# A decode layer on one core: w_down in five transfers instead of nine

## The chip, the cores and the metric

The kernel runs on one core of a Trainium2 chip. The metric is the device time of one execution in microseconds (us). A core has a tensor engine (PE in the profile's rows), a vector engine (DVE), a scalar engine (ACT), GpSimd (POOL) and SyncE (SP), each with its own instruction queue; weight loads of the tensor engine stand apart as PEld. All data comes by transfers that an engine's queue issues and sixteen transfer engines carry out, each with a share of every large transfer.

## The reference

One token passes a layer whose attention and gated MLP run in parallel on the same normalised input. All numbers are 32-bit floats. Attention looks at the last 4096 of 65536 cached positions, with 32 query heads on 4 key and value heads of 128.

```
def reference(A_x, A_k_cache, A_v_cache, A_wq, A_wo, B_x, B_w_gate, B_w_up, B_w_down):
    ...
        scores = jnp.einsum("bhqd,bhkd->bhqk", q, k) * (Dh ** -0.5)
        p = _softmax(scores, axis=-1)
        o = jnp.einsum("bhqk,bhkd->bhqd", p, v)
    ...
        g = jnp.einsum("bsd,df->bsf", x, w_gate)
        u = jnp.einsum("bsd,df->bsf", x, w_up)
        h = _gelu(g) * u
        return jnp.einsum("bsf,fd->bsd", h, w_down)
    ...
    xn = _layernorm(x, axis=-1)
    return x + _A_ref(xn, A_k_cache, A_v_cache, A_wq, A_wo) + _B_ref(xn, B_w_gate, B_w_up, B_w_down)
```

What matters here is the last product: a hidden vector h of 3584 numbers times w_down, 3584 x 1024, 14.7 MB.

## The kernel before, in words

Weights and caches are read once, 94 MB in all, and pass through one buffer of 176 KB in each of 128 partitions, `ring`. The list `pieces` names every transfer in order: its kind (q, k, v, g, u, o for the matrices and caches, d for w_down), which part, the place in `ring` in KB and the size in KB a partition. `pump` issues transfers from SyncE in that order, each as soon as no live piece holds its place; a piece ends with `done`. Which instruction waits for what is worked out by `Program.add` from overlapping places, piece of memory by piece of memory, so a transfer waits for the last readers of the bytes that it overwrites.

The vector by matrix products are shared between the two engines. w_down is cut into 28 tiles of 128 rows and 1024 columns (4 KB a partition each). `hz` holds h, one column a tile; `column(t)` is that column among zeros. A tile can be done in three ways:

- `tile_on_dve`: one instruction on the vector engine, `part = part + tile * column` (line 213), for the tile numbers in lists such as `HID_B`.
- `tiles_on_rows` and `tile_on_pe`: four or eight matmul calls a tile on the tensor engine. `tile_on_pe` cuts the 1024 columns into four blocks of 256 and sums into the bank `sums`; each call shows as two matmul records in the trace, so a tile is eight records.
- `half_on_pe`: half of a tile's columns, in four calls of 128 columns (eight records), into the bank `acc`.

All matmul calls stand on line 158, all vector additions on 189, all transfers on 219. `contract` does a whole piece: it gives its listed tiles to the vector engine and the others to the tensor engine.

The tail of the program, around the change: the two pieces of wo, "o" 0 and "o" 1, are done, each half on either engine. Then w_down: piece (0, 12) of 48 KB takes the place that the last piece of w_up left; all others go to the first 64 KB of `ring`, which "o" 0 leaves. (0, 12) is summed by rows in `acc` and on the vector engine in `part`; the vector engine adds `acc` to `part`. Then (12, 20), (20, 22), (22, 24), tile 24, a pass `tile_on_pe(unit, out_part)` that takes the vector engine's sum across the partitions into `sums`, and tile 25 last in `sums`. The vector engine adds `sums` to `x_out`, which holds x. Tiles 26 and 27 go in halves to `acc`: both halves of 26, then half 0 of 27, its addition to `x_out` and the store, then half 1 of 27, its addition and its store. Tile 27 comes in two transfers, one a half.

```
HID_B = [1, 3, 5, 7]
HID_C = []
HID_D = [1]
...
        ("d", (0, 12), 128, 48), ("d", (12, 20), 0, 32), ("d", (20, 22), 32, 8),
        ("d", (22, 24), 40, 8), ("d", (24, 25), 48, 4), ("d", (25, 26), 52, 4),
        ("d", (26, 27), 56, 4), ("d", (27, 28), 60, 4),
```

Of the kernel before, what the change touches and what calls it, by code (L numbers as in the profile page):

```python
# [10 lines left out]
P = 128  # L11
D = 1024
# [4 lines left out]
NQ = 512  # L17
NG = 448
TO = 16
TD = DF // P  # L20
# [7 lines left out]
HEADS_A = [0, 2, 4, 6, 8, 10, 12, 14]  # L28
HEADS_B = [0, 2, 4, 6, 8, 10, 12, 14]
HID_A = [0, 2, 4, 6, 8]  # L30
HID_B = [1, 3, 5, 7]
HID_C = []
HID_D = [1]


class Program:
# [110 lines left out]
def decode_layer(nc, x, k_cache, v_cache, wq, wo, w_gate, w_up, w_down, out):  # L147
    prog = Program(nc)

    def sbuf(name, *shape):  # L150
        return nc.alloc_sbuf_tensor(name, list(shape), F32)
# [4 lines left out]
    def mm(o, lhsT, rhs, start, stop, parts=None):  # L156
        prog.add(
            "pe", lambda e: e.matmul(o, lhsT, rhs, start=start, stop=stop),  # L158
            [lhsT] + (parts or [rhs]), [o],
        )  # L160
# [27 lines left out]
    def add(o, a, b):  # L188
        dve(lambda e: e.tensor_add(o, a, b), [a, b], [o])  # L189
# [27 lines left out]
    def dma(engine, o, i, reads=(), writes=(), tag=None):  # L217
        return prog.add(
            engine, lambda e: e.dma_start(o, i), list(reads), list(writes), dma=True, tag=tag  # L219
        )  # L220
# [4 lines left out]
    def rows(w, a):  # L225
        return w[512 * a:512 * (a + 1), :].rearrange("(p r) n -> p (r n)", r=4)

    def heads_of(a):
        return wo[2048 * a:2048 * (a + 1), :].rearrange("(p t) n -> p (t n)", p=P)

    hidden_rows = w_down.rearrange("(p t) n -> p t n", p=P)


    pieces = [
# [6 lines left out]
    ]  # L241
    held = {}

    def load(kind, i, at, size):
        slot = ring[:, at * KB:(at + size) * KB]
        held[kind, i] = slot
        if kind == "v":
            src = v_cache[0, 2 * i:2 * i + 2, SK - WIN:, :].rearrange("g (p j) d -> p g (j d)", p=P)
            dma("sp", slot.rearrange("p (g n) -> p g n", g=2), src, writes=[slot], tag=(kind, i))
        elif kind == "k":  # L250
            src = k_cache[0, 2 * i:2 * i + 2, SK - WIN:, :].rearrange("g (s j) d -> s g (j d)", g=2, j=64)
            dma("sp", slot, src, writes=[slot], tag=(kind, i))
        elif kind == "d":
            lo, hi = i
            halves = 2 if lo == TD - 1 else 1
            wide = slot.rearrange("p (t n) -> p t n", n=D)
            for half in range(halves):
                cols = slice(half * D // halves, (half + 1) * D // halves)
                dst = wide[:, :, cols]
                dma("sp", dst, hidden_rows[:, lo:hi, cols], writes=[dst], tag=(kind, i, half))  # L260
        else:
            src = {
                "q": lambda: rows(wq, i), "g": lambda: rows(w_gate, i), "u": lambda: rows(w_up, i),
                "o": lambda: heads_of(i),
            }[kind]()
            dma("sp", slot, src, writes=[slot], tag=(kind, i))
# [4 lines left out]
    def pump():  # L271
        while queue:
            kind, i, at, size = queue[0]
            if any(at < hi and lo < at + size for lo, hi in live.values()):
                return
            load(*queue.pop(0))
            live[kind, i] = (at, at + size)

    def done(*key):
        del live[key]  # L280
        pump()
# [8 lines left out]
    for k in range(2):  # L290
        dst = x_out[31 + 64 * k:33 + 64 * k, :, :]
# [22 lines left out]
    unit = sbuf("unit", P, 64)  # L314
# [133 lines left out]
    p = rows_sb[:, 0, :]  # L448
# [152 lines left out]
    out_part = part[:, :D]  # L601
# [3 lines left out]
    def column(t):  # L605
        return hz[:, 32 * t:32 * t + 64]

    def head(t):
        return oz[:, 32 * t:32 * t + 64]

    def tiles_on_rows(pairs):

        for at in range(0, len(pairs), 4):
            group = pairs[at:at + 4]
            for f in range(2):
                for k, (z, w) in enumerate(group):
                    c = (state["turn"] + k) % 4
                    first = (c, f) not in state["rows"]
                    state["rows"].add((c, f))
                    mm(  # L620
                        acc[32 * c:32 * c + 32, f, :], z[:, 31:63], w[:, f * NQ:(f + 1) * NQ],
                        first, state["turn"] + k >= state["total"] - 4,
                    )
            state["turn"] += len(group)

    def tile_on_pe(wide, w, stop=False):
        blocks = w.rearrange("p (f c n) -> p c f n", f=2, c=4)
        for c in range(4):
            at = 31 * (c % 2)
            mm(  # L630
                sums[32 * c:32 * c + 32, :].rearrange("p (f n) -> p f n", f=2),
                wide[:, at:at + 32], blocks[:, c], state["fresh"], stop,
            )
        state["fresh"] = False

    def half_on_pe(wide, w, half, first, last):
        for c in range(4):
            at = 31 * (c % 2)
            mm(
                acc[32 * c:32 * c + 32, half, :P],  # L640
                wide[:, at:at + 32], w[:, half * NQ + c * P:half * NQ + (c + 1) * P], first, last,
            )

    def tile_on_dve(z, w):
        add_scaled(out_part, w, z[:, 31:32], state["part"])
        state["part"] = False

    def contract(kind, i, z, dve_tiles, rows):
        w = held[kind, i].rearrange("p (t n) -> p t n", n=D)
        count = w.shape[1]  # L650
        rest = [(z(t), w[:, t, :]) for t in range(count) if t not in dve_tiles]
        if rows:
            tiles_on_rows(rest)
        else:
            for pair in rest:
                tile_on_pe(*pair)
        for t in dve_tiles:
            tile_on_dve(z(t), w[:, t, :])
        done(kind, i)
# [39 lines left out]
    state["total"] = 2 * TO + 12 - len(HEADS_A + HEADS_B + HID_A)  # L699
    contract("o", 0, head, HEADS_A, True)  # L700
    contract("o", 1, lambda t: head(TO + t), HEADS_B, True)
    contract("d", (0, 12), column, HID_A, True)
    add(out_part, acc[:].rearrange("p a n -> p (a n)"), out_part)
    contract("d", (12, 20), lambda t: column(12 + t), HID_B, False)
    contract("d", (20, 22), lambda t: column(20 + t), HID_C, False)
    contract("d", (22, 24), lambda t: column(22 + t), HID_D, False)
    tile_on_pe(column(24), held["d", (24, 25)])
    tile_on_pe(unit[:], out_part)
    tile_on_pe(column(25), held["d", (25, 26)], True)
    add(x_out[:].rearrange("p f n -> p (f n)"), sums[:], x_out[:].rearrange("p f n -> p (f n)"))  # L710
    for half in range(2):
        half_on_pe(column(26), held["d", (26, 27)], half, True, False)
    stores = out.rearrange("a b (f c n) -> (a b) f c n", f=2, c=4)
    for half in range(2):
        half_on_pe(column(27), held["d", (27, 28)], half, False, True)
        add(y[:, half, :], acc[:, half, :P], x_out[:, half, :])
        for k, engine in enumerate(("sp", "act")):
            src = y[31 + 64 * k:33 + 64 * k, half, :]
            dma(
                engine, stores[0, half, 2 * k:2 * k + 2, :], src, reads=[src],  # L720
                tag=("out", half, k),
            )
# [25 lines left out]
```

## Time and profile before

| what | value |
|---|---|
| median of three runs | 226.62 us (226.55 to 226.67) |
| the profiled execution, its own time | 226.83 us |
| its span, first to last instruction | 225.5 us |
| bytes read, over the span | 94.38 MB, 419 GB/s |
| mean granted clock of the tensor engine | 0.803 of 2.4 GHz |

The span leaves out 1.3 us around the instructions. A row of the timeline gives the start of a run of like instructions, its length, engine, source line, operation, what is written and read, the count, and in brackets how long the engine stood idle before it and what ended that. A wait for a transfer ends when the last of the sixteen engines has reported its share.

### The profile page before, as it was taken

The numbers are of one execution on the slowest core, as the hardware profiler recorded it, in microseconds if no ns is written. First come the engines' busy times: TensorE is split into PE (matmuls) and PEld (weight loads), VectorE is DVE, ScalarE is ACT, GpSimd is POOL, SyncE is SP. The second block draws the span as 40 slices with busy tenths as digits, with TensorE's granted clock in tenths as the row PEclk, the third lists the DMA queues.
The fourth block names the chain that finished last, engine by engine and source line by source line (L and its number), as shares of the span: only waits on it lengthen the run. The fifth ranks groups of instructions, "written<-read, shape, count | busy, mean of one in ns | idle before, by whom it ended". The sixth has DMA issues, their size and how long they took to land.

```text
span 225.5 us, 1396 instructions
## 1 busy us (share of the span) xinstructions
PE 87.5 (39%) x574; PEld 34.8 (15%) x574; DVE 143.2 (64%) x127; ACT 26.3 (12%) x45; POOL 0.7 (0%) x6
## 2 busy tenths in 40 slices
PE   1200000007699007989002537137339204408475
PEld 0100000006263002462000111011002001002131
DVE  7500998499727990000998699869538804938691
ACT  2000000004555001482000300200000000000000
POOL 1000000000000000000000000000000000000000
PEclk9999999999999755999755667857855855965889
DMA  9899899899989999999999998999999999999992
GB/s 373 372 395 535 372 395 535 349 405 478 468 349 426 465 401 503 427 397 471 427 397 392 433 509 387 478 391 491 419 395 488 419 395 413 427 439 442 382 405 111
DMA packets 3317, 94.46 MB, mean 419 GB/s; under 512 B 350, under 2 KB 366, under 8 KB 1008
## 3 DMA queue, kind: packets, MB, share of 16 engines
q1 hardware_dynamic: 3288, 94.38, 97.5%
q8 instruction: 4, 0.07, 0.1%
q10 hardware_dynamic: 24, 0.01, 0.0%
q14 instruction: 1, 0.01, 0.0%
HBM read 94.38 MB, written 0.00 MB: 419 GB/s over the span
## 4 chain that ended last, share of the span: by engine, by line
DMA 65%; DVE 26%; PE 7%; issue 1%; SPq 1%; DVEq 0%
DVE part L213 24%; DMA ring<-in_B_w_down 19%; DMA ring<-in_A_wq 18%; DMA ring<-in_B_w_gate 15%; DMA ring<-in_A_wo 13%; PE acc L158 3%; PE tp L163 2%; PE s_p L158 2%; DVE part L209 1%; SPq L219 1%; DVE rows_sb L186 0%; DVE part L189 0%; DVEq L118 0%; SPq L118 0%
## 5 line engine op out<-in xcount | busy, mean ns | idle before, releaser
L213 DVE SCALAR_TENSOR_TENSOR part<-ring,xz,part 128x3584 f32<-128x3584 f32 (+1 forms) x19 | 78.8, 4148 | 26.6 <-DMA ring<-in_B_w_gate 22.6
L163 PE MATMUL tp<-ident,ring 128*128 128x128 f32 x128 | 20.3, 303 | 44.4 <-DMA ring<-in_A_k_cache 42.8
L213 DVE SCALAR_TENSOR_TENSOR part<-ring,oz,part 128x1024 f32<-128x1024 f32 x15 | 19.3, 1285 | 9.9 <-DMA ring<-in_A_wo 9.4
L172 ACT ACTIVATE ring<-tp 128x512 f32<-128x512 f32 x32 | 18.1, 596 | 58.4 <-PE tp L163 58.0
L163 PEld LDWEIGHTS tp<-ident,ring 128*128 128x128 f32 x128 | 15.0, 152 | 51.2 <-DMA ring<-in_A_k_cache 42.9
L209 DVE TENSOR_SCALAR part<-ring,xz 128x3584 f32<-128x3584 f32 (+1 forms) x3 | 6.5, 2176 | 19.7 <-DMA ring<-in_A_wq 12.1
L158 PE MATMUL acc<-ring,oz 128*32 128x512 f32 x64 | 11.7, 899 | 16.8 <-DMA ring<-in_A_wo 16.8
L213 DVE SCALAR_TENSOR_TENSOR part<-ring,hz,part 128x1024 f32<-128x1024 f32 x10 | 12.8, 1285 | 6.1 <-DMA ring<-in_B_w_down 5.8
L158 PE MATMUL acc<-part,unit 128*32 128x448 f32 (+1 forms) x48 | 7.3, 742 | 22.3 <-DVE part L213 22.3
L158 PE MATMUL o_p<-ring,pT 128*32 128x512 f32 x64 | 11.0, 847 | 7.1 <-DMA ring<-in_A_v_cache 6.5
L158 PE MATMUL acc<-ring,hz 128*32 128x128 f32 (+1 forms) x60 | 8.0, 616 | 10.1 <-DMA ring<-in_B_w_down 10.1
L158 PE MATMUL s_p<-ring,qz 128*32 128x512 f32 x64 | 9.3, 598 | 0.0
L163 PE MATMUL tp<-ident,rows_sb 128*128 128x128 f32 x16 | 3.5, 361 | 12.0 <-ACT rows_sb L172 11.8
L158 PE MATMUL sums<-ring,hz 128*32 128x256 f32 x72 | 6.2, 482 | 4.7 <-DMA ring<-in_B_w_down 4.7
L158 PEld LDWEIGHTS acc<-ring,oz 128*32 128x32 f32 x64 | 2.5, 155 | 26.6 <-DMA ring<-in_A_wo 19.4
L158 PEld LDWEIGHTS acc<-part,unit 128*32 128x32 f32 x48 | 1.4, 126 | 26.4 <-DVE part L213 24.2
L172 ACT ACTIVATE rows_sb<-s_p,negm 128x512 f32<-128x512 f32 x2 | 1.4, 687 | 30.4 <-DVE negm L209 30.4
L158 PEld LDWEIGHTS o_p<-ring,pT 128*32 128x32 f32 x64 | 2.6, 149 | 14.5 <-issue 13.4
L158 PE MATMUL acc<-ring,xz 128*32 128x448 f32 x32 | 4.8, 767 | 0.0
L158 PEld LDWEIGHTS acc<-ring,hz 128*32 128x32 f32 x60 | 2.2, 135 | 15.8 <-issue 14.0
L163 PEld LDWEIGHTS tp<-ident,rows_sb 128*128 128x128 f32 x16 | 2.3, 179 | 15.5 <-ACT rows_sb L172 13.6
L158 PEld LDWEIGHTS sums<-ring,hz 128*32 128x32 f32 x72 | 2.4, 136 | 9.2 <-DMA ring<-in_B_w_down 7.3
(85 smaller groups left out, 47.8 us busy)
## 6 DMA issues: line engine op xcount, KB each, us to landing
ring<-in_B_w_gate SPq DMA_DIRECT2D x2, 7168.0 KB, 31.9
ring<-in_B_w_up SPq DMA_DIRECT2D x2, 7168.0 KB, 33.9
ring<-in_A_k_cache SPq DMA_DIRECT2D x2, 4096.0 KB, 39.7
ring<-in_A_v_cache SPq DMA_DIRECT2D x2, 4096.0 KB, 34.8
ring<-in_B_w_down SPq DMA_DIRECT2D x1, 6144.0 KB, 42.9
ring<-in_B_w_down SPq DMA_DIRECT2D x1, 4096.0 KB, 38.8
ring<-in_B_w_down SPq DMA_DIRECT2D x2, 1024.0 KB, 40.4
ring<-in_B_w_down SPq DMA_DIRECT2D x3, 512.0 KB, 42.0
```

Source lines behind the costliest of these rows:

```text
L158: "pe", lambda e: e.matmul(o, lhsT, rhs, start=start, stop=stop),
L163: prog.add("pe", lambda e: e.transpose(o, i, eye), [i, eye], [o])
L172: "act", lambda e: e.activation(o, i, func, scale=scale, **kw),
L209: dve(lambda e: e.tensor_scalar(o, i, s1, s2, op0=op0, **kw), reads, [o])
L213: lambda e: e.scalar_tensor_tensor(o, i, factor, other, op0=ALU.mult, op1=ALU.add),
L219: engine, lambda e: e.dma_start(o, i), list(reads), list(writes), dma=True, tag=tag
```

## The change

The same bytes of w_down come in five transfers instead of nine. Pieces are now named in half tiles of 512 columns. (0, 24) is the old first piece, 48 KB. (24, 44) has ten tiles, 12 to 21, 40 KB. (44, 52) has tiles 22 to 25, 16 KB. (52, 55) has tile 26 and the first half of 27, 6 KB; (55, 56) has the second half, 2 KB. The vector engine does three of the ten tiles of the second piece and nothing after it, where it did four of (12, 20) and one of (22, 24). Tiles 22 to 25 no longer go by `tile_on_pe` to `sums` but in halves to `acc`, ahead of 26 and 27; `tile_on_pe(unit, out_part)` is the last into `sums`. Both halves of tile 26 are done when their own half of the output is.

```
-HID_B = [1, 3, 5, 7]
-HID_C = []
-HID_D = [1]
+HID_B = [1, 3, 5]
...
-        ("d", (0, 12), 128, 48), ("d", (12, 20), 0, 32), ("d", (20, 22), 32, 8),
-        ("d", (22, 24), 40, 8), ("d", (24, 25), 48, 4), ("d", (25, 26), 52, 4),
-        ("d", (26, 27), 56, 4), ("d", (27, 28), 60, 4),
+        ("d", (0, 24), 128, 48), ("d", (24, 44), 0, 40), ("d", (44, 52), 40, 16),
+        ("d", (52, 55), 56, 6), ("d", (55, 56), 62, 2),
...
+            dma("sp", slot, hidden_halves[:, lo * NQ:hi * NQ], writes=[slot], tag=(kind, i))
...
-    def half_on_pe(wide, w, half, first, last):
+    def half_on_pe(t, half, first, last):
+
+        h = 2 * t + half
+        lo, hi = next(i for kind, i in held if kind == "d" and i[0] <= h < i[1])
+        w = held["d", (lo, hi)][:, (h - lo) * NQ:(h - lo + 1) * NQ]
...
-    contract("d", (12, 20), lambda t: column(12 + t), HID_B, False)
-    contract("d", (20, 22), lambda t: column(20 + t), HID_C, False)
-    contract("d", (22, 24), lambda t: column(22 + t), HID_D, False)
-    tile_on_pe(column(24), held["d", (24, 25)])
-    tile_on_pe(unit[:], out_part)
-    tile_on_pe(column(25), held["d", (25, 26)], True)
+    contract("d", (24, 44), lambda t: column(12 + t), HID_B, False)
+    tile_on_pe(unit[:], out_part, True)
     add(x_out[:].rearrange("p f n -> p (f n)"), sums[:], x_out[:].rearrange("p f n -> p (f n)"))
     for half in range(2):
-        half_on_pe(column(26), held["d", (26, 27)], half, True, False)
+        for t in range(22, 26):
+            half_on_pe(t, half, t == 22, False)
...
     for half in range(2):
-        half_on_pe(column(27), held["d", (27, 28)], half, False, True)
+        half_on_pe(26, half, False, False)
+        half_on_pe(27, half, False, True)
```

The tensor engine's instructions from the second piece of w_down to the end, first before the change. Each row is a run of like matmul calls, with the semaphores that the first one waits for; s_dma440 to s_dma447 are the transfers after the 48 KB in order, s_dve is the vector engine.

```order
L158 MATMUL sums<-ring,hz 32x256 [waits s_dma440]
L158 MATMUL sums<-ring,hz 32x256 x15
L158 MATMUL sums<-ring,hz 32x256 [waits s_dma441]
L158 MATMUL sums<-ring,hz 32x256 x7
L158 MATMUL sums<-ring,hz 32x256 [waits s_dma442]
L158 MATMUL sums<-ring,hz 32x256 x3
L158 MATMUL sums<-ring,hz 32x256 [waits s_dma443]
L158 MATMUL sums<-ring,hz 32x256 x3
L158 MATMUL sums<-part,unit 32x256 [waits s_dve]
L158 MATMUL sums<-part,unit 32x256 x3
L158 MATMUL sums<-ring,hz 32x256 [waits s_dma444]
L158 MATMUL sums<-ring,hz 32x256 x3
```

After these stand the halves of tiles 26 and 27: eight calls behind s_dma445, four behind s_dma446, four behind s_dma447. The same stretch with the change, to the end of the program; s_dma440 to s_dma443 are now the 40, 16, 6 and 2 KB.

```order
L156 MATMUL sums<-ring,hz 32x256 [waits s_dma440]
L156 MATMUL sums<-ring,hz 32x256 x27
L156 MATMUL sums<-part,unit 32x256 [waits s_dve]
L156 MATMUL sums<-part,unit 32x256 x3
L156 MATMUL acc<-ring,hz 32x128 [waits s_dma441]
L156 MATMUL acc<-ring,hz 32x128 x31
L156 MATMUL acc<-ring,hz 32x128 [waits s_dma442]
L156 MATMUL acc<-ring,hz 32x128 x11
L156 MATMUL acc<-ring,hz 32x128 [waits s_dma443]
L156 MATMUL acc<-ring,hz 32x128 x3
```

The first row behind each wait counts with the run under it: 28 calls are seven tiles, 32 calls of 128 columns are eight halves. Of the twelve calls behind s_dma442, four are half 1 of tile 26.

## Rows read from the trace of the kernel before

**Rows 1.** The page: busy us, share of the span, instructions; then the load queue.
```profile
PE 87.5 (39%) x574; PEld 34.8 (15%) x574; DVE 143.2 (64%) x127; ACT 26.3 (12%) x45; POOL 0.7 (0%) x6
...
q1 hardware_dynamic: 3288, 94.38, 97.5%
```

**Rows 2.** The chain that ended last, its end: start, us, what.
```profile
180.50 42.73 DMA ring<-in_B_w_down
223.23 0.04 issue
223.28 0.47 PE acc L158 x8
223.75 0.02 issue
223.77 0.29 DVE part L189
```

**Rows 3.** The timeline of the tail, tensor and vector engine.
```profile
189.00 5.29 PE L158 MATMUL acc<-ring,oz 128*32 128x512 f32 x32 [12.93 <-DMA ring<-in_A_wo]
...
203.59 6.57 DVE L213 SCALAR_TENSOR_TENSOR part<-ring,hz,part 128x1024 f32<-128x1024 f32 x5 [4.00 <-DMA ring<-in_B_w_down]
...
203.63 6.50 PE L158 MATMUL acc<-ring,hz 128*32 128x512 f32 x28 [9.33 <-DMA ring<-in_B_w_down]
...
213.25 4.26 PE L158 MATMUL sums<-ring,hz 128*32 128x256 f32 x48 [3.12 <-DMA ring<-in_B_w_down]
213.30 6.57 DVE L213 SCALAR_TENSOR_TENSOR part<-ring,hz,part 128x1024 f32<-128x1024 f32 x5 [1.82 <-DMA ring<-in_B_w_down]
...
218.22 0.64 PE L158 MATMUL sums<-ring,hz 128*32 128x256 f32 x8 [0.71 <-DMA ring<-in_B_w_down]
...
219.49 0.64 PE L158 MATMUL sums<-ring,hz 128*32 128x256 f32 x8 [0.62 <-DMA ring<-in_B_w_down]
...
220.78 0.64 PE L158 MATMUL sums<-ring,hz 128*32 128x256 f32 x8 [0.21 <-DMA ring<-in_B_w_down]
...
222.03 1.04 PE L158 MATMUL acc<-ring,hz 128*32 128x128 f32 x24 [0.61 <-DMA ring<-in_B_w_down]
222.64 0.16 PEld L158 LDWEIGHTS acc<-ring,hz 128*32 128x32 f32 x8 [0.24 <-DMA ring<-in_B_w_down]
...
223.28 0.43 PE L158 MATMUL acc<-ring,hz 128*32 128x128 f32 x8 [0.21 <-DMA ring<-in_B_w_down]
```

**Rows 4.** The timeline, SyncE: issues of w_down's transfers after the first.
```profile
174.37 17.02 SPq L219 DMA_DIRECT2D ring<-in_B_w_down  x8
```

**Rows 5.** The timeline, weight loads of the burst at 213.25: one row a group.
```profile
213.68 0.20 PEld L158 LDWEIGHTS sums<-ring,hz 128*32 128x32 f32 x4 [0.23 <-issue]
214.11 0.20 PEld L158 LDWEIGHTS sums<-ring,hz 128*32 128x32 f32 x4 [0.23 <-issue]
214.53 0.20 PEld L158 LDWEIGHTS sums<-ring,hz 128*32 128x32 f32 x4 [0.23 <-issue]
```

**Rows 6.** The timeline from 222.03 to 222.62: both halves of tile 26.
```profile
222.03 0.64 PE L158 MATMUL acc<-ring,hz 128*32 128x128 f32 x16 [0.61 <-DMA ring<-in_B_w_down]
```

**Rows 7.** Stretches, tensor engine: from:to, us, busy (count), granted clock, transfers' share, GB/s.
```profile
86.81:89.99 3.18, 3.18 (x16) 0.50 1.26 544
122.73:127.53 4.80, 4.26 (x20) 0.50 1.02 433
133.45:137.77 4.32, 4.32 (x24) 0.50 0.98 425
151.53:154.84 3.31, 3.31 (x21) 0.50 0.82 356
169.65:175.32 5.67, 5.67 (x28) 0.50 1.04 451
189.00:192.39 3.39, 3.39 (x16) 0.50 1.04 449
203.63:209.45 5.82, 5.82 (x25) 0.50 0.98 422
213.25:216.28 3.03, 3.03 (x32) 0.50 0.99 410
216.28:217.52 1.24, 1.24 (x24) 1.00 1.02 406
```

More of the change, by code (lines that the diff above doesn't have):

```diff
@@ L229, in heads_of @@
         return wo[2048 * a:2048 * (a + 1), :].rearrange("(p t) n -> p (t n)", p=P)
-    hidden_rows = w_down.rearrange("(p t) n -> p t n", p=P)
+    hidden_halves = w_down.rearrange("(p t) n -> p (t n)", p=P)
     pieces = [
@@ L254, in load @@
             lo, hi = i
[L255 to L260, printed above, removed]
+            dma("sp", slot, hidden_halves[:, lo * NQ:hi * NQ], writes=[slot], tag=(kind, i))
         else:
@@ L640, in half_on_pe @@
                 acc[32 * c:32 * c + 32, half, :P],
-                wide[:, at:at + 32], w[:, half * NQ + c * P:half * NQ + (c + 1) * P], first, last,
+                column(t)[:, at:at + 32], w[:, c * P:(c + 1) * P], first, last,
             )
@@ L701, in decode_layer @@
     contract("o", 1, lambda t: head(TO + t), HEADS_B, True)
-    contract("d", (0, 12), column, HID_A, True)
+    contract("d", (0, 24), column, HID_A, True)
     add(out_part, acc[:].rearrange("p a n -> p (a n)"), out_part)
-    contract("d", (12, 20), lambda t: column(12 + t), HID_B, False)
-    contract("d", (20, 22), lambda t: column(20 + t), HID_C, False)
-    contract("d", (22, 24), lambda t: column(22 + t), HID_D, False)
-    tile_on_pe(column(24), held["d", (24, 25)])
-    tile_on_pe(unit[:], out_part)
-    tile_on_pe(column(25), held["d", (25, 26)], True)
+    contract("d", (24, 44), lambda t: column(12 + t), HID_B, False)
+    tile_on_pe(unit[:], out_part, True)
     add(x_out[:].rearrange("p f n -> p (f n)"), sums[:], x_out[:].rearrange("p f n -> p (f n)"))
     for half in range(2):
-        half_on_pe(column(26), held["d", (26, 27)], half, True, False)
+        for t in range(22, 26):
+            half_on_pe(t, half, t == 22, False)
     stores = out.rearrange("a b (f c n) -> (a b) f c n", f=2, c=4)
     for half in range(2):
-        half_on_pe(column(27), held["d", (27, 28)], half, False, True)
+        half_on_pe(26, half, False, False)
+        half_on_pe(27, half, False, True)
         add(y[:, half, :], acc[:, half, :P], x_out[:, half, :])
```

## Prediction

> **What bounds the kernel now.** I read the page first [rows 1]: the vector engine is busy for 143.2 us of the span of 225.5, the tensor engine for 87.5, and the packets of the one load queue for 97.5% of what sixteen transfer engines have. So the transfers set the pace, and an engine costs time only at the end. The chain that ended last [rows 2] says where that end is: a wait for w_down to 223.23, then 0.47 us on TensorE, 0.29 us on VectorE, and the stores until 225.5. Then I read the tail in order of time [rows 3], each row a burst that starts when a piece lands. TensorE starts at 203.63 on the 48 KB, at 213.25 on the 32 KB, then at 218.22, 219.49, 220.78, 222.03, 222.64 and 223.28. Before each of these it was waiting for a transfer: it keeps up with the pieces, and what is left after the last one is half a tile.
>
> **Part 1: fewer transfers.** The pace of a large piece: 203.59 - 189.00 = 14.59 us for 48 KB a partition, and 213.25 - 203.59 = 9.66 us for 32 KB, so 0.303 us a KB. By that pace 4 KB take 1.21 us; the single tiles landed 1.27, 1.29 and 1.25 us apart [rows 3], so one more transfer costs about 0.05 us. The two of 8 KB took 4.97 us where the pace gives 4.85, which is 0.06 each. The last 64 KB come in eight transfers now and in four after, so four go: 4 x 0.05 = **0.20 us**. Bounds: nothing if the price goes by bytes alone, and 0.29 us if all that the 64 KB lose to the pace (223.28 - 203.59 = 19.69 against 19.40) were given back. I take 0.20 because single tiles are nearest to what goes. A loss is excluded here: the bytes and the transfer engines are the same.
>
> The landings after are then 215.7 (203.59 + 40 x 0.303) for 40 KB, 220.6 (16 x 0.303 + 0.05 later) for 16 KB, 222.45 for 6 KB, 223.1 for 2 KB.
>
> The Trainium skill ("DMA: Bandwidth & Descriptors", section "Anatomy of one DMA") gives each transfer a fixed cost of about 2.0 us beside its bytes. Paid one after another, four fewer would be worth 8 us, not 0.2. The rows speak against that here: three transfers of 512 KB landed under 1.3 us apart.
>
> The second piece needs 40 KB of the ring instead of 32, so its issue waits for two more tiles of wo. That is hidden: the eight issues now lie between 174.37 and 191.39 [rows 4], and the last of them is still 12 us ahead of the end of the 48 KB at 203.59, behind which they all queue. The four issues that go were on SyncE, which nobody waits for there.
>
> **Part 2: TensorE's work is bunched.** VectorE gives two tiles (1.3 us each, off the path) to TensorE. More important is when TensorE gets work. Now it has four tiles of the 32 KB and two of the next 8 KB from 213.25 on, and then one tile at a time. After the change it has nothing from 210.13 (203.63 + 6.50) to 215.7, and then, in order: seven tiles of the 40 KB, the pass over VectorE's sum (as long as a tile), tiles 22 to 25 as eight halves, two halves of tiles 26 and 27 (half 0), two more (half 1). Two halves are a tile, so that is 7 + 1 + 4 + 1 + 1 = 14 tiles.
>
> A tile at the low clock: its two groups of four matmuls start 0.43 us apart (213.68, 214.11, 214.53 [rows 5]), so 0.85 us. A half tile at the high clock: the burst of two takes 0.64 us [rows 6] and that of one 0.43 [rows 3], so 0.21 us, and 0.43 us a tile, half as long as at the low clock. Fourteen tiles are 14 x 0.43 = 6.0 us at the high clock, and each us at the low clock loses half a us.
>
> Which clock? At 213.25, after 3.1 us without work, the burst began at 1.2 GHz and was granted 2.4 GHz only at 216.28 [rows 7]. After the change the engine will have been idle for 5.6 us, so I take 1.2 GHz as certain at 215.7. How long it lasts is the term with the widest bounds. Eight bursts of this trace that began at 1.2 GHz stayed there for 3.18, 4.80, 4.32, 3.31, 5.67, 3.39, 5.82 and 3.03 us [rows 7] (each row runs from the burst's first matmul to the rise); their mean is 4.2 us, which I take, with 3.0 and 5.8 as bounds. Call it L.
>
> The Trainium skill ("TensorE: Matmul & The Clock Gate", Part 1) says that the throttled state is the default and that the point of its release varies from run to run for one kernel. The scatter within this trace agrees; that it varies between runs no run here shows.
>
> **The sum.** TensorE gets through its work at 215.7 + 6.0 + L/2 = 221.7 + L/2. Before, it was through at 223.28 + 0.21 = 223.49. So the end moves by L/2 - 1.8 us, but never to before the last piece: 223.1 + 0.21 = 223.3, which is -0.20. At L = 4.2 that is **+0.3 us**. What follows (0.28 us until VectorE starts, its 0.29 us, the store) stays as it is: half 0 is added and stored under half 1's matmuls. VectorE's three tiles end at 215.7 + 3.9 = 219.6; TensorE asks for their sum at 215.7 + 3.0 + L/2 = 220.8 or, with L at its lowest, 220.2, so that wait costs nothing. A half tile loads weights as often as a whole one; the burst of rows 6, two halves, has those loads in its 0.64 us.
>
> Against its own time the profiled execution would go from 226.83 to about 227.15. That execution stands 0.21 us above the median of the runs, 226.62, so I forecast 226.62 + 0.3, rounded to **226.95 us**.
>
> **The rivals.**
> 1. The end stays with the transfers. If the clock rises within about 3.2 us, TensorE is through before the last 2 KB and only part 1 counts: 226.62 - 0.20 = 226.42. For it: two of the eight bursts (3.03 and 3.18) were that short. Against it: the other six.
> 2. **Slower: the clock rises late.** It decides from L = 4.5 on, where L/2 - 1.8 passes 0.45 us. Place: the chain from the landing at 215.7 through the seven tiles to half 1. Price: at 5.67 and 5.82, as after the idle stretches before 169.65 and 203.63, it is 2.85 - 1.8 = +1.05 and +1.1, so about 227.7. For it: three of eight bursts were over 4.5, and the burst on the 48 KB, 12 us earlier, was the longest of all. Against it: the burst on the 32 KB, the one nearest in place, was the shortest.
> 3. Each transfer holds the queue for a fixed time, whatever its size, and the bytes go faster than part 1 has it. The two halves of the last tile landed 0.61 and 0.64 us apart (222.03, 222.64, 223.28), so that time is at most 0.61 us, and four fewer are worth at most 2.4 us: 224.2, if TensorE's backlog does not take it back. It passes -0.45 us from 0.11 us a transfer on. For it: nothing in rows 3. Against it: 4 KB take twice as long as 2 KB, and 32 KB nearly eight times as long as 4 (9.66 us against 1.27). By the 2.0 us that the Trainium skill's page on DMA gives (an estimate, 4 x 2.0 = 8) it would be 218.6.
> 4. The change does not do what it says, because the 40 KB are issued too late for the queue to stay full. It would cost what the queue runs dry; against it stand the 12 us of rows 4. I give it nothing of its own.
>
> **How the numbers follow.** A difference of 0.2%, 0.45 us, is about what a measurement of this kernel can tell from no change. The forecast (L from 3.2 to 4.5: -0.2 to +0.45): 0.42. Rival 1: 0.15. Rival 2: 0.38; the three of eight bursts are 0.375, and a median over a few runs pulls that neither way by much. Rival 3, with any other gain beyond part 1: 0.05. So within 0.2%: 0.42 + 0.15 = 0.57; slower 0.38; faster 0.05. The range has rival 1 at its low end, 226.4, and at its high end most of rival 2: 226.62 + 1.0 = 227.6; it leaves out rival 3 and the latest rises. The likeliest case's own range is 226.4 to 227.07.
>
> **What would show it.** The five pieces should release TensorE near 203.6, 215.7, 220.6, 222.45 and 223.1, or the last two should find it still busy, with no wait for a transfer before half 1. The granted clock should be 1.2 GHz from 215.7 for 3 to 6 us. The chain that ended last should go from w_down through TensorE for several us, not 0.47, if the backlog decides; if it still shows the wait for w_down and half a us of TensorE, rival 1 is right. The forecast is wrong if the burst begins at 2.4 GHz, if landings are over 0.3 us off, or if a tile costs other than 0.85 and 0.43 us.

## The result, and the profile after

The change made the kernel slower by about half a microsecond, 0.2%: 227.24 us median (226.50 to 227.81, 22 runs) against 226.68 (226.55 to 227.00, 22 runs of the kernel before beside them); ratio 1.0021, 95% interval 1.0013 to 1.0029, which is +0.48 us with +0.3 to +0.7 around it. That stands on the 0.2% line and not clear of it. What changed more than the middle is the scatter: 0.45 us wide before, 1.3 us after. The spans scatter likewise: 225.2 to 225.6 us in 29 runs of the kernel before (those beside the first experiments), 225.0 to 226.5 after.

The profiled execution took 227.67 us, its span is 226.3. The page, in the order of [rows 1]:

```profile
PE 90.9 (40%) x622; PEld 38.2 (17%) x622; DVE 140.7 (62%) x125; ACT 25.9 (11%) x45; POOL 0.7 (0%) x6
...
q1 hardware_dynamic: 2712, 94.37, 97.0%
```

Nothing to see there but 576 packets fewer. The end of the chain that ended last, as [rows 2], tells the change:

```profile
175.66 39.92 DMA ring<-in_B_w_down
215.57 0.04 issue
215.62 6.33 PE sums L156 x64
221.95 2.67 PE acc L156 x96
224.62 0.02 issue
224.64 0.29 DVE part L187
```

The chain leaves the transfers at 215.57, when the 40 KB land, and then runs on TensorE for 9.0 us. Before, it stayed with the transfers until 223.23 and had 0.47 us of TensorE. The timeline of TensorE's tail, against [rows 3]:

```profile
203.58 5.52 PE L156 MATMUL acc<-ring,hz 128*32 128x512 f32 x28 [8.62 <-DMA ring<-in_B_w_down]
215.62 5.90 PE L156 MATMUL sums<-ring,hz 128*32 128x256 f32 x56 [6.52 <-DMA ring<-in_B_w_down]
221.34 0.60 PE L156 MATMUL sums<-part,unit 128*32 128x256 f32 x8
221.77 2.79 PE L156 MATMUL acc<-ring,hz 128*32 128x128 f32 x96
```

The bracket ahead of 215.62 has 6.52 us without work. The next two rows have no bracket: TensorE waited for nothing from there to the end, neither for the 16, the 6 and the 2 KB nor for VectorE's sum. Before, every TensorE row of [rows 3] began with a wait. The stretches, with the columns of [rows 7] (from:to, us, busy (count), granted clock, transfers' share, GB/s):

```profile
209.10:210.84 1.74, 0.00 (x0) 1.00 0.87 377
210.84:214.25 3.41, 0.00 (x0) 1.00 0.84 360
214.25:215.62 1.37, 0.00 (x1) 0.50 0.95 407
215.62:221.08 5.46, 5.46 (x52) 0.50 0.92 379
221.08:224.56 3.48, 3.48 (x112) 1.00 0.11 41
```

The level fell from 2.4 to 1.2 GHz at 214.25, with the engine idle since 209.10, and rose again at 221.08, 5.46 us into the burst. In those 5.46 us, 52 records of 256 columns were begun, six and a half of the fourteen tiles; the other seven and a half took 3.48 us at 2.4 GHz.

### The profile page after: what moved, and what is told of

It is laid out like the page before. It is cut to its first block, busy times and chain, and to the rows that moved or that the text cites. A ratio compares the mean times of both kernels' runs of the same rounds, so it can differ in the third digit from the quotient of the medians.

```text
span 226.3 us, 1484 instructions
## 1 busy us (share of the span) xinstructions
PE 90.9 (40%) x622; PEld 38.2 (17%) x622; DVE 140.7 (62%) x125; ACT 25.9 (11%) x45; POOL 0.7 (0%) x6
## 4 chain that ended last, share of the span: by engine, by line
DMA 72%; DVE 16%; PE 10%; ACT 1%; issue 0%; DVEq 0%
DMA ring<-in_A_v_cache 18%; DMA ring<-in_B_w_down 18%; DMA ring<-in_B_w_gate 14%; DVE part L211 14%; DMA ring<-in_A_wo 13%; DMA ring<-in_A_wq 10%; PE o_p L156 5%; PE sums L156 3%; DVE part L207 2%; PE acc L156 1%; PE tp L161 1%; ACT rows_sb L170 0%; DVE m L199 0%; ACT pT L170 0%; DVE part L187 0%
## 5 line engine op out<-in xcount | busy, mean ns | idle before, releaser
L156 PE MATMUL acc<-part,unit 128*32 128x448 f32 (+1 forms) x48 | 9.6, 948 | 19.7 <-DVE part L211 19.7
L211 DVE SCALAR_TENSOR_TENSOR part<-ring,hz,part 128x1024 f32<-128x1024 f32 x8 | 10.3, 1285 | 8.5 <-DMA ring<-in_B_w_down 8.3
L156 PE MATMUL o_p<-ring,pT 128*32 128x512 f32 x64 | 12.3, 938 | 8.0 <-DMA ring<-in_A_v_cache 7.3
L156 PEld LDWEIGHTS acc<-ring,hz 128*32 128x32 f32 x124 | 4.0, 120 | 12.9 <-issue 12.8
L156 PE MATMUL acc<-ring,xz 128*32 128x448 f32 x32 | 5.7, 893 | 0.0
## 6 DMA issues: line engine op xcount, KB each, us to landing
ring<-in_B_w_down SPq DMA_DIRECT2D x1, 5120.0 KB, 39.9
ring<-in_B_w_down SPq DMA_DIRECT2D x1, 2048.0 KB, 42.2
ring<-in_B_w_down SPq DMA_DIRECT2D x1, 768.0 KB, 42.7
```

The lines of the kernel that those rows point to most:

```text
L211: lambda e: e.scalar_tensor_tensor(o, i, factor, other, op0=ALU.mult, op1=ALU.add),
```

## The experiments

All are the changed kernel with one edit, except where it says so. The two theories: the **clock theory** of the prediction, that the end moves by L/2 - 1.8 us, not below -0.2, where L is the time that the burst on the 40 KB stays at 1.2 GHz; and **bunching**, that fourteen tiles behind one landing are too many at any clock.

**The changed kernel twice more** (no edit), for further pairs of L and span.

> The changed kernel once more, for another pair of L (how long the burst at 215.6 stays at 1.2 GHz) and span. Theory: span = 225.5 + L/2 - 1.8, not under 225.3. Rival (the clock does not matter): the spans scatter without regard to L.

> The changed kernel a third time, for a further pair of L and span. Theory: span = 225.5 + L/2 - 1.8, not under 225.3. Rival: no relation.

The stretches at the low and then at the high clock, first run and second run:

```profile
215.69:219.45 3.76, 3.76 (x36) 0.50 0.99 413
219.45:223.80 4.35, 4.35 (x128) 1.00 0.39 151
```

```profile
215.62:219.69 4.07, 4.07 (x40) 0.50 0.97 405
219.69:223.88 4.19, 4.19 (x124) 1.00 0.36 138
```

| run | L, us | span by 225.5 + L/2 - 1.8 | span measured |
|---|---|---|---|
| first repeat | 3.76 | 225.6 | 225.6 |
| second repeat | 4.07 | 225.7 | 225.7 |
| profile of the result | 5.46 | 226.4 | 226.3 |

One kernel, three executions, three different L, and the span goes with L. Three points are few, but the burst began at the same time in all three (215.62 to 215.69) on the same fourteen tiles, so bunching has nothing to explain the 0.7 us between them. L itself is not a property of the kernel: the same burst stayed slow for 3.76 to 5.46 us.

**Extra work in the idle stretch, too much of it.** Calls are put between the 48 and the 40 KB, into a bank that nothing reads, so that TensorE is not idle.

```
     add(out_part, acc[:].rearrange("p a n -> p (a n)"), out_part)
+    for k in range(12):
+        for c in range(4):
+            mm(s_p[32 * c:32 * c + 32, :], unit[:, 0:32], held["d", (0, 24)][:, :NQ], True, True)
```

> The changed kernel, and 48 extra matmul calls of 512 columns (12 groups of four) on TensorE between the 48 KB piece and the 40 KB piece, into a bank that nothing reads; the output does not hang on them. At 0.43 us a group at the high clock they fill 5.2 of the 5.5 to 6.5 us in which TensorE had no work. Theory (the backlog costs because the burst at 215.6 begins at 1.2 GHz): the burst now begins at 2.4 GHz, the fourteen tiles are done at 215.6 + 6.0 = 221.6, the transfers end it, and the time is 0.2 us under the kernel before, about 226.45, with a scatter no wider than that of the kernel before (0.45 us). Rival (the bunching itself costs, fourteen tiles after one landing, whatever the clock): as the changed kernel, about 227.2 with a scatter of 1.3 us. If the extra calls run at the low clock they end late and the time rises above 227.2.

Measured: 228.87 us (228.44 to 229.43, 5 runs), ratio 1.0097, 95% interval 1.0084 to 1.0110. The expectation missed, and its price was wrong: four calls show as eight records, and eight of 512 columns take 0.86 us at the high clock, so 48 calls took 10.4 us, not 5.2, and the tiles of the 40 KB began at about 219.9 instead of 215.6. (The "four or eight matmul calls a tile" of the kernel's description are records too: `tiles_on_rows` does a tile in two calls, `tile_on_pe` in four.) The run still holds a measurement:

```profile
209.37:219.80 10.43, 10.43 (x104) 1.00 0.93 392
219.87:226.34 6.47, 6.47 (x161) 1.00 0.21 81
```

The granted clock was 2.4 GHz throughout, and the fourteen tiles, their drain with them, took 6.5 us. That is near the 6.0 us of the prediction's sum for all work at the high clock; the end of the last matmuls adds some 0.2.

**Extra work, half of it.** As above with `range(6)`; run in two series.

> As the run with 48 extra calls, with 24: they showed eight records, not four, to 0.86 us at the high clock, so 24 calls fill 5.2 us, from about 209.4 to 214.6, and end ahead of the 40 KB at 215.6. Nothing that the output needs hangs on them. Theory: the burst at 215.6 begins at 2.4 GHz, the fourteen tiles are done by about 221.8, before the last 2 KB at 223.0, and the time is 226.45 (0.2 us under the kernel before), the slowest run under 227. Rival (bunching, whatever the clock): 227.2, slowest 227.8, as the changed kernel.

> The run with 24 extra calls once more, for a second interval beside the same runs of the kernel before. Theory: 0.2 us under the kernel before (ratio 0.999), slowest run under 227. Rival (the first interval was chance): ratio 1.000 or above.

Measured: 226.57 us (226.38 to 226.90, 11 runs), ratio 0.9989, 95% interval 0.9980 to 0.9998; and the second time 226.67 (226.44 to 226.87, 11 runs), ratio 0.9995, interval 0.9986 to 1.0004. The second interval takes in no change. The stretches of the first, two of the second, then the timeline of the first one's tail:

```profile
209.26:215.00 5.74, 5.74 (x54) 1.00 0.88 374
215.62:218.85 3.23, 3.23 (x56) 1.00 0.96 408
218.85:223.44 4.59, 3.56 (x105) 1.00 0.51 202
```

```profile
213.75:215.66 1.91, 0.00 (x1) 1.00 0.89 377
215.66:218.89 3.23, 3.23 (x56) 1.00 0.98 413
```

```profile
215.62 3.23 PE L156 MATMUL sums<-ring,hz 128*32 128x256 f32 x56 [0.62 <-DMA ring<-in_B_w_down]
219.66 0.64 PE L156 MATMUL sums<-part,unit 128*32 128x256 f32 x8 [0.80 <-DVE part L211]
220.52 2.92 PE L156 MATMUL acc<-ring,hz 128*32 128x128 f32 x96 [0.22 <-DMA ring<-in_B_w_down]
```

The seven tiles that took 5.90 us now take 3.23, at the same landing, with the same fourteen tiles behind it. TensorE is ahead again: it waits 0.80 us for VectorE's sum and 0.22 us for the 16 KB. The slowest of all 22 runs took 226.90, where the changed kernel had 13 of 22 over 227.1; the mean spans are 225.25 and 225.30 us against its 225.74. This decides between the two theories: the work was bunched as before, only the clock differed, and the loss is gone with its scatter. Bunching falls.

It is also the one version below the kernel before, by 0.22 and 0.14 us on the medians. That is too little to call faster; it is about what the prediction has the transfers save.

**The transfers of the kernel before, the work as changed.** Nine transfers, three tiles on VectorE, tiles 22 to 25 in halves.

```
-        ("d", (0, 24), 128, 48), ("d", (24, 44), 0, 40), ("d", (44, 52), 40, 16),
-        ("d", (52, 55), 56, 6), ("d", (55, 56), 62, 2),
+        ("d", (0, 24), 128, 48), ("d", (24, 40), 0, 32), ("d", (40, 44), 32, 8),
+        ("d", (44, 48), 40, 8), ("d", (48, 50), 48, 4), ("d", (50, 52), 52, 4),
+        ("d", (52, 54), 56, 4), ("d", (54, 55), 60, 2), ("d", (55, 56), 62, 2),
...
-    contract("d", (24, 44), lambda t: column(12 + t), HID_B, False)
+    contract("d", (24, 40), lambda t: column(12 + t), HID_B, False)
+    contract("d", (40, 44), lambda t: column(20 + t), [], False)
```

> The transfers of the kernel before (48, 32, 8, 8, 4, 4, 4, 2, 2 KB), with the changed kernel's split and order of the work: three tiles on VectorE after the 48 KB, tiles 22 to 25 in halves. Theory (the late start after the merged 40 KB makes the backlog): TensorE starts at 213.25, is through its backlog by 219.3 + L/2, at most 222.2, and the transfers end it as before: 226.6 to 226.7, no difference, scatter as before. Rival (the two tiles moved from VectorE and the order in halves cost): some 0.3 to 0.6 us over the kernel before.

Measured: 226.83 us (226.69 to 227.05, 11 runs), ratio 1.0005, 95% interval 0.9997 to 1.0014, scatter 0.36 us. No difference that can be told, as the theory has it: two tiles more on TensorE and the new order cost nothing while the pieces land as before. The last row of its tail begins with a wait again:

```profile
222.71 1.06 PE L156 MATMUL acc<-ring,hz 128*32 128x128 f32 x24 [0.21 <-DMA ring<-in_B_w_down]
```

**The 40 KB cut again, 32 and 8** (and the second `contract` as above).

> The changed kernel with the 40 KB cut again into 32 and 8 (six transfers: 48, 32, 8, 16, 6, 2). Theory: TensorE starts at 213.25 instead of 215.6, the backlog is done by 219.3 + L/2, under 222.3 for every L seen, and three transfers fewer are worth 3 x 0.05 = 0.15 us: about 226.5, scatter as before. Rival (small transfers cost nothing, and the landing of the 16 KB at 220.5 is what is late): 226.65 or above, up to 227.2.

Measured: 226.92 us median, but 226.48 to 228.26 in 12 runs, ratio 1.0027, 95% interval 1.0008 to 1.0045. The expectation missed: five of the twelve runs lie between 228.0 and 228.3, and none between 227.0 and 228.0. The median lies in the rival's range, but the rival has no two groups. The profiled execution was one of the five long ones (228.26 us); two rows of its timeline, then its stretches:

```profile
213.19 3.56 PE L156 MATMUL sums<-ring,hz 128*32 128x256 f32 x56 [3.86 <-DMA ring<-in_B_w_down]
...
220.60 4.49 PE L156 MATMUL acc<-ring,hz 128*32 128x128 f32 x96 [2.74 <-DMA ring<-in_B_w_down]
```

```profile
213.19:216.75 3.56, 3.44 (x56) 1.00 1.04 440
217.90:220.55 2.65, 0.00 (x0) 1.00 0.92 372
220.60:221.55 0.95, 0.94 (x36) 1.00 0.44 175
221.55:224.96 3.41, 3.41 (x72) 0.50 0.09 31
```

After 3.86 us without work the burst at 213.19 ran at 2.4 GHz from its start, so TensorE was done early with the 40 KB and, but for the pass over VectorE's sum, idle until the 16 KB landed, the last 2.65 us without a break. Its burst on the 16 KB began at 2.4 GHz and fell to 1.2 in the middle, at 221.55, for the 3.41 us that held nearly all that was left. So the idle stretch was not removed but split, and its second part lies where even less time is left to make it good. By the half us lost for each us at the low clock, 3.41 us cost 1.7, and the spans of the five long runs (226.7 to 226.9) lie 1.1 to 1.7 us over those of the others (225.2 to 225.6). The two groups of runs fit executions in which the level fell there and others in which it did not; only one of the long ones was profiled, so for the others this is argued.

**The 40 KB cut into 20 and 20** (two tiles of the first and one of the second on VectorE).

```
-        ("d", (0, 24), 128, 48), ("d", (24, 44), 0, 40), ("d", (44, 52), 40, 16),
+        ("d", (0, 24), 128, 48), ("d", (24, 34), 0, 20), ("d", (34, 44), 20, 20), ("d", (44, 52), 40, 16),
...
+    contract("d", (24, 34), lambda t: column(12 + t), [1, 3], False)
+    contract("d", (34, 44), lambda t: column(17 + t), [1], False)
```

> The changed kernel with the 40 KB cut into 20 and 20 (six transfers: 48, 20, 20, 16, 6, 2); VectorE does two tiles of the first and one of the second. Theory: the first 20 KB land at 209.6, as TensorE ends the 48 KB, so three tiles go before the idle stretch, and ten tiles and the sum's pass are left at 215.65: 215.65 + 4.7 + L/2 = 220.4 + L/2, which passes the end of the transfers (223.2) only for L over 5.7. About 226.5, with at most 0.1 us more in the slowest runs. Rival (any idle stretch ahead of the last 40 KB costs): part of the 0.5 us stays, 226.8 to 227.0.

Measured: 226.77 us (226.47 to 227.50, 11 runs), ratio 1.0001, 95% interval 0.9992 to 1.0010. The loss is gone, the gain did not come, and the scatter of 1.0 us is more than expected. In its profile the second 20 KB began at 1.2 GHz too, but with three tiles less to do and an L of 2.73 us the burst was through before the 16 KB landed:

```profile
215.52:218.25 2.73, 2.73 (x28) 0.50 0.94 401
218.25:219.20 0.95, 0.95 (x20) 1.00 1.01 420
219.20:220.39 1.19, 0.00 (x1) 1.00 0.93 380
220.39:223.34 2.95, 2.95 (x96) 1.00 0.30 118
```

That execution is the longest of the eleven, 227.50 us, and yet its span is 225.1: 2.4 us lie outside the instructions, where the kernel before has 1.3. The next longest, 227.11, has a span of 225.1 too. All eleven spans lie between 225.1 and 225.6, so the long runs are not TensorE's doing; what fills the time outside, no trace shows.

**One tile more on VectorE, and its sum taken later.**

```
-HID_B = [1, 3, 5]
+HID_B = [1, 3, 5, 7]
...
-    tile_on_pe(unit[:], out_part, True)
-    add(x_out[:].rearrange("p f n -> p (f n)"), sums[:], x_out[:].rearrange("p f n -> p (f n)"))
     for half in range(2):
         for t in range(22, 26):
             half_on_pe(t, half, t == 22, False)
+    tile_on_pe(unit[:], out_part, True)
+    add(x_out[:].rearrange("p f n -> p (f n)"), sums[:], x_out[:].rearrange("p f n -> p (f n)"))
```

> The changed kernel with a fourth tile of the 40 KB on VectorE (six on TensorE), and the pass over VectorE's sum moved behind tiles 22 to 25, since that sum now ends at 215.67 + 5.24 = 220.9. Theory: one tile less is 0.43 us less of TensorE's work, so the end moves by L/2 - 2.2 against the kernel before, not below -0.2: 226.4 to 227.3, median about 226.6. Rival (bunching, or the landings): median no more than 0.1 us under the changed kernel's 227.24. Second rival (VectorE's sum is late now): TensorE shows a wait for VectorE behind tiles 22 to 25.

Measured: 227.22 us (226.86 to 227.48, 11 runs) beside 226.79 for the kernel before, ratio 1.0022, 95% interval 1.0013 to 1.0031. The expectation missed: the median is where the first rival had it, at most 0.1 us under the changed kernel's 227.24. But the run changes two things, and the second one undid the first, so it decides nothing between the theories. The pass over the sum now stands behind the landing of the 16 KB, so seven tiles are left there instead of six:

```profile
215.85 5.05 PE L156 MATMUL sums<-ring,hz 128*32 128x256 f32 x48 [6.93 <-DMA ring<-in_B_w_down]
220.85 1.95 PE L156 MATMUL acc<-ring,hz 128*32 128x128 f32 x64
222.60 0.64 PE L156 MATMUL sums<-part,unit 128*32 128x256 f32 x8
223.03 1.08 PE L156 MATMUL acc<-ring,hz 128*32 128x128 f32 x32
```

From 220.85 on it has 7 x 0.43 = 3.0 us of work at the high clock, to about 223.9, and no wait for VectorE. Had it stood ready when the 16 KB landed (at about 220.5 in the run with 24 extra calls), it would have been through at 223.5, however small L is, which is where the kernel before is through. So nothing could be gained, which fits a lowest run of 226.86. The rest of the median is open; in this profile the 40 KB released TensorE at 215.85, 0.2 us later than in the other runs, and the burst stayed low for 4.63 us:

```profile
215.85:220.48 4.63, 4.62 (x44) 0.50 0.97 403
```

**Eighteen transfers more** (the kernel before, with its 48 and 32 KB in pieces of 4 KB; the work stays).

```
-            for half in range(halves):
+            for t in range(hi - lo if hi <= 20 else 1):
+                n = 1 if hi <= 20 else hi - lo
+                for half in range(halves):
...
```

> The kernel before, with its 48 and 32 KB of w_down cut into twenty transfers of 4 KB (27 transfers of w_down instead of nine); the work and its order stay. Theory (part 1: one more transfer costs about 0.05 us of the queue, TensorE is in time): 18 x 0.05 = 0.9 us more, 227.6 to 227.7. Rival (a price per transfer of 0.11 us or more): 2 us more or over. Second rival (bytes alone): no difference.

Measured: 228.05 us (227.98 to 228.54, 6 runs) beside 226.81, ratio 1.0059, 95% interval 1.0047 to 1.0071: +1.34 us for eighteen transfers, 0.074 us each (0.059 to 0.089). That is nearer to the 0.05 of the prediction than to either rival, but the interval leaves out all three. In its timeline three single tiles begin 1.28 us apart, 0.07 over the pace of large pieces; the last row is the weight load of the last half tile:

```profile
201.67 1.05 PE L158 MATMUL acc<-ring,hz 128*32 128x512 f32 x2 [0.66 <-DMA ring<-in_B_w_down]
202.95 1.05 PE L158 MATMUL acc<-ring,hz 128*32 128x512 f32 x2 [0.23 <-DMA ring<-in_B_w_down]
204.23 1.48 PE L158 MATMUL acc<-ring,hz 128*32 128x512 f32 x7 [0.23 <-DMA ring<-in_B_w_down]
...
224.49 0.16 PEld L158 LDWEIGHTS acc<-ring,hz 128*32 128x32 f32 x8 [0.21 <-DMA ring<-in_B_w_down]
```

TensorE was not quite in time here: it was at 1.2 GHz from about 210.8 to 224.4, and the chain that ended last leaves the transfers at 220.63 and runs over TensorE. So the 1.34 us need not be the queue's alone. The last half tile still waited for its landing, until 224.49 where it was 223.28 before: 1.21 us later, 0.067 us for each of eighteen.

## Why the prediction was right, and where it was off

**What bounds the kernel.** Right for the tail, which is all that the runs touched: the transfers set the pace there, and TensorE costs time where work is left behind the last landings. That no engine costs time earlier rests on the 97.5% of the load queue and was not tested. The kernel before was waiting for transfers again from 218.22 on, and with its transfers and the changed work TensorE still waited at 222.71: little work follows each of the last pieces.

**Part 1, fewer transfers.** The landings came as worked out. The trace of the changed kernel has the last four issued at 175.66, 178.30, 179.62 and 180.00 us and landed 39.9, 42.2, 42.7 and 43.0 us later: at 215.6, 220.5, 222.3 and 223.0, for 215.7, 220.6, 222.45 and 223.1. The last one is 0.2 us ahead of the 223.23 before, which is the gain that was forecast. The price of a transfer was mis-sized a little: 0.05 us forecast, 0.067 by the landings and 0.074 by the times measured, so four are worth 0.2 to 0.3 us. The fixed 2.0 us that the Trainium skill ("DMA: Bandwidth & Descriptors", "Anatomy of one DMA") gives each transfer stands there for transfers that GpSimd issues, and these are SyncE's. In this queue no such cost shows: eighteen more cost 1.34 us, not 36.

**Part 2, the backlog.** Right in every step that a row shows: idle to 215.6, then 1.2 GHz, no wait from there to the end, 6.0 us of work at the high clock, half a us lost for each us at the low one. The three spans follow the formula to 0.1 us, and its bounds are those of the runs: -0.2 us and +1.1 us of 226.68 are 226.5 and 227.8, and the 22 runs went from 226.50 to 227.81. That they meet to a hundredth is luck, since the kernel before alone scatters by 0.45. The low level at 215.6, called certain from one stretch of 3.1 us without work, came in all three profiles after 5.5 to 6.5 us. As a rule the step was too strong: with 32 and 8 KB, 3.86 us without work left the burst at 2.4 GHz.

**The size of L.** The number was 0.29 us too low: 226.95 forecast, 227.24 measured, above the likeliest case's own range (to 227.07) and inside the full one (to 227.6). The prediction took 4.2 us for L, the mean of eight bursts of one trace; the three profiles gave 3.76, 4.07 and 5.46, mean 4.4. By the formula the measured +0.48 us stands for 2 x (0.48 + 1.8) = 4.6 us, and the medians' +0.56 for 4.7. But not all of the 0.48 is L. The mean span of the 22 runs is 225.74 us, that of the 29 runs of the kernel before 225.42: +0.32, which stands for 4.2. The rest, 0.1 to 0.2 us, lies outside the instructions, about half of it in two runs (227.52 us with a span of 225.3, and 227.06 with 225.1), and its cause stays open. So L was a little short or right. What was too low is the chance of a late rise: 0.38 was given, and 13 of 22 runs were more than 0.45 us over the median of the kernel before, eleven of them with spans of 225.9 us and more.

**The rivals.** The first, an end that stays with the transfers, is what some five of the runs were by their times (226.50 to 226.67); none of them was profiled. The second is what most were, and where the median lies. The third fell with the 0.074 us, whose interval ends at 0.089, short of 0.11. That the change might not do what it says never came up: the 40 KB were issued at 175.66 and landed on time.

The Trainium skill ("TensorE: Matmul & The Clock Gate", Part 1) says that the point at which the throttle is released varies from run to run of one kernel. The three traces of the changed kernel agree: it rose 3.76, 4.07 and 5.46 us after the same first matmul.

## What to carry to other kernels

Before merging the last transfers of a stream, look at what the engine behind them does meanwhile: a small saving in the queue (here 0.07 us a transfer) is lost again if the engine idles, drops to its low clock and then has more work left than the transfers still last. Work out that backlog at both clock levels and with the low level held as long as any burst of the trace held it; a scatter that grows between runs is a sign of it. Compare spans as well as times: time outside the instructions can pass for a loss of the engine. Removing one idle stretch can open another later, as the 32 and 8 KB showed, so look for the next one before measuring.

## What was not expected of the hardware

- The level can fall in the middle of a burst: with 32 and 8 KB, TensorE idled from 217.90 to 220.55 at a granted 2.4 GHz, took up work, and was at 1.2 GHz only from 221.55 on, 0.95 us into it, for 3.41 us.
- The length of the idle stretch did not settle the level. After 3.12 us without work the kernel before began at 1.2 GHz (213.25); after 3.86 us the run with 32 and 8 KB began at 2.4 (213.19).
- One kernel's times split into two groups in that run, 226.5 to 227.0 and 228.0 to 228.3. The one long execution that was profiled shows the fall; for the others it is not shown.
- Work that nobody needs can pay for itself: 24 calls into an unused bank held 2.4 GHz (1.00 in all three stretches) and took the seven tiles from 5.90 to 3.23 us.
